# Moving the jobs that prepare sums of w2, and giving eight stores to ScalarE, in a fused attention and mixture-of-experts kernel

## The chip, the cores and the metric

One core of one Trainium2 chip. The metric is the device time of one execution in microseconds; the time of a kernel is the median over its runs. A core has five engines with a queue of instructions each: TensorE (PE; PEld is its loading of weights), VectorE (DVE), ScalarE (ACT), GpSimd (POOL) and SyncE (SP). In this kernel SP only issues DMA transfers; GpSimd issues some as well.

## The reference

Two parts, the output of the first being the input of the second. Attention goes through 32 memory slots per head (8 batches, 8 heads, 576 rows, 64 columns); then come four experts (512 → 1024 → 512), each weighted by a probability per row.

```python
a = softmax(phi, over the sequence)
k_m = einsum('bhsm,bhsd->bhmd', a, k)
v_m = einsum('bhsm,bhsd->bhmd', a, v)
attn = softmax(q @ k_m^T / sqrt(64))
x = (attn @ v_m), heads side by side        # 4608 x 512
p = domain_probs / (sum of domain_probs + 1e-9)
for e in range(4):
    h = maximum(x @ w1[e], 0)
    out += p[:, e:e+1] * (h @ w2[e])
```

## The kernel before

**Precision.** Every fp32 operand of a matmul is split into two parts: ScalarE copies (rounds) the high one, and DVE or GpSimd subtracts to get the low one. A product is then three matmuls. In the trace these splits are `L156`/`L157` (w1, w2, v), `L351`/`L352` (k and v), `L659`/`L661` (the hidden block `h`).

**Stages.** The batches are taken in four pairs. The product x·w1 is not formed from x: v_m·w1 (`vw`, L560/L562) is formed per head and expert, and the transposed attention `AT` is multiplied by it. Pairs 0 and 1 run as 256 steps, 128 to a pair (`PAIR`), 32 to an expert. A step makes one hidden block and uses another:

```python
for s in range(a, b):
    accumulate()
    run_plan(s)
    first(s + AHEAD)
    second(s)
```

`first` (L647 to L661) makes the hidden block of two steps later: matmuls, the rectified high part on ScalarE (L659), the low part on DVE (L661). `second` (L680 to L682) multiplies the step's block by a block of w2. `run_plan(s)` runs whatever was put at step s with `at(s, ...)`: the attention of later batches, the splits of the next expert's weights, loads and stores. Pairs 2 and 3 run afterwards as 64 units in another scheme with seven products in place of eight; these need sums and differences of the quadrants of w2, split in two parts.

**Order.** Steps 0 to 35 are ordered by the compiler's scheduler. From step 36 (`FREE`) on the order is that of the code: on every engine an instruction stands where `run_plan` wrote it, and an engine executes its instructions in that order.

**The jobs.** Eight jobs (one for each expert and half of its hidden width; `JOBS`, function `sums`) prepare those quadrant sums during the steps. A job at step s has SP load two blocks of w2 of 512 KB into a tile `raw` (L208), DVE form the sums from step s+3 on (L231 to L234), ScalarE copy the high parts into `sv` (L220) and GpSimd subtract the low ones (L221), four of each; and GpSimd issue four stores to memory (L226). The jobs have no tiles of their own. They borrow the attention's: `raw` lies in the tile of tag "a" and `sv` in those of "tl" and "ph", except job 5, which takes one of three "AT" tiles and one of the "kvs" tiles. A tile is handed on when its last user is done; the next job's load therefore waits for the previous job's stores.

**Keeping w2.** `keep_w2(e, j)` stores the split blocks of w2 (512 KB each) at steps 20 to 27 of every expert in the first pair (L184, issued by GpSimd); the second pair loads them back (`load_w2`, L193, issued by SP, `w<-kw` in the trace).

**Attention of batch b** (`ATT`): the first number is the step of the load of phi, the second the step in which v_m is written.

Throughout, "job n" counts from 0, "P+61" is step 61 of the second pair, and `kw` and `v` in the order are the stores' places in memory.

Of the kernel before, what the change touches and what calls it, by code (L numbers as in the profile page):

```python
# [9 lines left out]
F32 = mybir.dt.float32  # L10
# [8 lines left out]
N, DM, E, F = 4608, 512, 4, 1024  # L19
P = 128  # L20
# [8 lines left out]
PAIR = E * STEPS  # L29
# [26 lines left out]
    4: (PAIR, PAIR + 35, (PAIR + 34, PAIR + 37, PAIR + 41), (PAIR + 38, PAIR + 42, PAIR + 45)),  # L56
    5: (PAIR + 26, PAIR + 53, (PAIR + 76, PAIR + 80, PAIR + 84), (PAIR + 112, PAIR + 113, PAIR + 114)),
    6: (PAIR + 40, PAIR + 67, (2 * PAIR + 23, 2 * PAIR + 27, 2 * PAIR + 31), (2 * PAIR + 29, 2 * PAIR + 33, 2 * PAIR + 37)),
    7: (PAIR + 62, PAIR + 88, (2 * PAIR + 98, 2 * PAIR + 102, 2 * PAIR + 106), (2 * PAIR + 115, 2 * PAIR + 116, 2 * PAIR + 117)),
}  # L60

UNITS_1 = (1, 5, 5, 6, 5, 6, 8, 9, 10, 11, 11, 12, 17, 13, 13, 20)
# [7 lines left out]
UNITS = (NG - SEVEN) * E * 2 * 4  # L70
Q = 256
X_BANK, Y_BANK, AB_BANK = 4, 2, 6
JOBS = (62, 87, 99, 108, 117, PAIR + 28, PAIR + 85, PAIR + 94)
KEEP_AT, W2_AGAIN = 20, 24
FOUR_AT_7 = ((0, 4, 8, 12), (16, 20, 24, 28))
VW_LOAD_7 = ((21, 37), (26, 41))
# [4 lines left out]
def body(ctx: ExitStack, tc: tile.TileContext, qm, qt, kv, kvt, phi, prob, w1, w1d, w2, out):  # L81
    nc = tc.nc
    pool = lambda name, **k: ctx.enter_context(tc.tile_pool(name=name, bufs=1, **k))
    const, wp, work, att = pool("const"), pool("wp"), pool("work"), pool("att")
    dram = pool("dram", space=DRAM)
# [67 lines left out]
    w1t, w2t = {}, {}  # L153
# [19 lines left out]
        w2t[k, e, j] = t  # L173

    kept_for = {}
    leaving = []

    def leave(key, t):
        leaving.append((key, t))

    def leave_now():
        for key, t in leaving:
            kept_for[key] = dram.tile([P, 2, DM], F32, name="k" + "".join(map(str, key)))
            nc.gpsimd.dma_start(kept_for[key], t.bitcast(F32))  # L184
        leaving.clear()

    def keep_w2(e, j):
        leave(("w2", e, j), w2t[0, e, j])
        leave_now()

    def load_w2(k, e, j):
        t = wp.tile([P, 2, DM], F32R, name="w2", tag="w2", bufs=NJ + 1)
        nc.sync.dma_start(t.bitcast(F32), kept_for["w2", e, j])  # L193
        w2t[k, e, j] = t

    def sums(s, own, e, fh):

        kept = []
        top, low = slice(0, Q), slice(Q, DM)
        sub, v = nc.vector.tensor_sub, nc.vector  # L200

        def load():
            tag = {"tag": "a"} if own else {"tag": "AT", "bufs": 3}
            t = att.tile([P, 2, 2, DM], F32R, name="raw", **tag)
            kept.extend(t[:, i].bitcast(F32) for i in range(2))
            kept.append(t)
            for i in range(2):
                nc.sync.dma_start(kept[i], w2[e, 2 * fh + i])  # L208

        def high(i, j):  # L210
            if j == 0:
                if own and i:
                    t = att.tile([P, 2, 640], F32R, name="sv", tag="ph")
                    t = t.rearrange("p a c -> p (a c)")[:, :2 * DM].rearrange("p (a c) -> p a c", a=2)
                elif own:
                    t = att.tile([P, 2, DM], F32R, name="sv", tag="tl")
                else:
                    t = att.tile([P, 2, DM], F32R, name="sv", tag="kvs", bufs=KVS)
                kept.append(t)
            nc.scalar.copy(kept[3 + i][:, j], kept[i][:, j])  # L220
            nc.gpsimd.tensor_sub(kept[2][:, i, j], kept[i][:, j], kept[3 + i][:, j].bitcast(F32))  # L221

        def store(i):
            d = dram.tile([P, 2, 2, DM], F32, name=f"v{e}{fh}{i}")
            for r, src in enumerate((kept[3 + i], kept[2][:, i])):
                nc.gpsimd.dma_start(d[:, :, r], src.bitcast(F32))  # L226
            for j in range(2):
                kept_for["v", e, fh, 2 * i + j] = d[:, j]

        at(s, load)  # L230
        at(s + 3, lambda: v.tensor_add(kept[1][:, :, low], kept[0][:, :, low], kept[1][:, :, low]))  # L231
        at(s + 3, lambda: sub(kept[0][:, :, low], kept[0][:, :, top], kept[0][:, :, low]))
        at(s + 4, lambda: sub(kept[0][:, :, top], kept[1][:, :, low], kept[0][:, :, top]))
        at(s + 4, lambda: sub(kept[1][:, :, top], kept[1][:, :, top], kept[0][:, :, top]))  # L234
        for i in range(2):
            for j in range(2):
                at(s + 4 + 2 * i + j, lambda i=i, j=j: high(i, j))
            at(s + 6 + 2 * i, lambda i=i: store(i))

    def units_w1(e, fh, g):  # L240
        kept = []
# [468 lines left out]
    def at(s, unit):  # L710
        plan[s].append(unit if isinstance(unit, tuple) else (None, unit))
# [76 lines left out]
    for k in range(NG):  # L788
        for e in range(E):
            s = k * PAIR + e * STEPS  # L790
# [34 lines left out]
    for e in range(E):  # L825
        for j in range(NJ):
            at(e * STEPS + KEEP_AT + j, lambda a=(e, j): keep_w2(*a))
    for n, s in enumerate(JOBS):
        sums(s, s != PAIR + 28, n // 2, n % 2)
    for s in FIRST_LOADS:  # L830
        at(s, lambda: load_part(wp.tile([P, 2, DM], F32R, name="w2", tag="w2", bufs=NJ + 1)))

# [17 lines left out]
    for block in range(UNITS // 4):  # L850
        e, fh = divmod(block % (2 * E), 2)
# [428 lines left out]
```

## Time and profile before

| | us |
|---|---|
| runs | 1407.55, 1407.58, 1413.63 |
| median | 1407.58 |
| the profiled execution | 1409.54 |
| its span | 1407.4 |
| TensorE busy in it | 1366.8 |
| VectorE busy | 837.9 |
| ScalarE busy | 624.8 |
| GpSimd busy | 621.4 |
| mean granted TensorE clock | 0.994 of full speed |

The span runs from the first to the last instruction of the profiled execution; its own time is 2.1 us longer, and the median of the runs is 2.0 below that. Steps 0 to 255 end at about 800 us; the 64 units fill the rest. A row of the timeline has the start in us, the duration (of a run of alike instructions, as "x8" tells, the stretch), the engine, the line, the operation, what is written and read with shapes, and in brackets the idle time of the engine before it with what ended it. `SPq` and `POOL ... DMA` rows are the issuing of transfers, not the transfers. A row of a window has its bounds and length, the busy time of PE, PEld, DVE, ACT and POOL with counts, the granted clock, the busy share of the DMA engines and GB/s.

### The profile page before, as it was taken

The page shows a single profiled execution, that of the slowest core. Times are in us where ns is not written, and L with a number is a line of the kernel's source. Part 1 is how long each engine was busy: PE and PEld are TensorE (multiplying, and loading weights), DVE is VectorE, ACT ScalarE, POOL GpSimd, SP SyncE. Part 2 cuts the span into 40 slices and gives each one's busy share as a digit, 9 for nine tenths or more (in the row PEclk, how much of TensorE's full clock was granted, in tenths as well). Part 3 has the DMA queues.
Part 4 walks back from the last instruction along what each step waited for, and adds up shares of the span by engine and source line. Part 5 has one row for each costly group of instructions (what it writes and reads, how often), then busy time and mean ns, then how long its engine had stood idle before and what let it go on. Part 6 is the DMA issues. An engine that isn't in the chain of part 4 may idle for free.

```text
span 1407.4 us, 25235 instructions
## 1 busy us (share of the span) xinstructions
PE 1366.8 (97%) x8894; PEld 1250.2 (89%) x8894; DVE 837.9 (60%) x1894; ACT 624.8 (44%) x1536; POOL 621.4 (44%) x660
## 2 busy tenths in 40 slices
PE   7899999999999999999979999999999999999998
PEld 6688888888878888889868999899999999999998
DVE  7775545446754365354434467777667666666665
ACT  7654555433444364463225354555543333333332
POOL 4410344755552334422245276676763334333333
PEclk9999999999999999999989999999999999999999
DMA  7832327799684264444588898999985776666662
GB/s 252 272 104 84 123 85 246 228 354 318 226 313 163 90 226 145 139 140 124 188 272 292 278 311 289 314 315 331 321 306 154 223 190 179 177 180 177 178 177 80
DMA packets 102029, 301.37 MB, mean 214 GB/s; under 512 B 24976, under 2 KB 26128, under 8 KB 101904
## 3 DMA queue, kind: packets, MB, share of 16 engines
q1 hardware_dynamic: 81168, 224.26, 51.3%
q0 software_dynamic: 20736, 75.51, 13.8%
q8 instruction: 71, 1.16, 0.4%
q14 instruction: 54, 0.44, 0.1%
HBM read 213.46 MB, written 84.93 MB: 212 GB/s over the span
## 4 chain that ended last, share of the span: by engine, by line
PE 58%; DMA 1%; DVE 1%; ACT 0%; issue 0%; POOL 0%; SPq 0%; DVEq 0%; ACTq 0%
PE banks L1008 22%; PE banks L922 5%; PE banks L923 5%; PE banks L924 5%; PE banks L682 3%; PE banks L680 3%; PE banks L681 3%; PE banks L585 2%; PE banks L647 2%; PE banks L648 2%; PE banks L649 2%; PE banks L1046 1%; PE banks L1047 1%; PE banks L1048 1%; PE banks L469 1%; PE banks L363 1%
## 5 line engine op out<-in xcount | busy, mean ns | idle before, releaser
L1026 DVE SCALAR_TENSOR_TENSOR acc<-banks,pt,acc 128x256 f32<-128x256 f32 x416 | 200.0, 481 | 108.9 <-PE banks L1008 105.2
L157 POOL TENSOR_TENSOR w<-stage,w 128x512 fp32r<-128x512 f32 x134 | 176.6, 1323 | 166.0 <-ACT w L156 153.9
L682 PE MATMUL banks<-w,h 128*128 128x512 f32 x512 | 201.9, 395 | 14.3 <-DVE h L661 14.3
L661 DVE SCALAR_TENSOR_TENSOR h<-banks,h 128x256 fp32r<-128x256 f32 x256 | 107.6, 420 | 164.3 <-ACT h L659 101.6
L680 PE MATMUL banks<-w,h 128*128 128x512 f32 x512 | 202.2, 395 | 1.7 <-DVE acc L702 1.3
L681 PE MATMUL banks<-w,h 128*128 128x512 f32 x512 | 201.7, 394 | 0.0
L659 ACT ACTIVATE h<-banks 128x256 fp32r<-128x256 f32 x256 | 97.8, 384 | 193.1 <-PE banks L649 152.2
L647 PE MATMUL banks<-AT,vw 128*128 128x256 f32 (+1 forms) x512 | 157.4, 308 | 5.7 <-ACT kvs L351 2.2
L1008 PE MATMUL banks<-w,a 128*128 128x256 f32 x1080 | 154.6, 282 | 0.3 <-DVE acc L1026 0.2
L648 PE MATMUL banks<-AT,vw 128*128 128x256 f32 (+1 forms) x512 | 151.7, 297 | 0.0
L922 PE MATMUL banks<-AT,vw 128*128 128x256 f32 (+1 forms) x512 | 151.6, 296 | 0.0
L649 PE MATMUL banks<-AT,vw 128*128 128x256 f32 (+1 forms) x512 | 151.2, 296 | 0.1
L923 PE MATMUL banks<-AT,vw 128*128 128x256 f32 (+1 forms) x512 | 151.1, 295 | 0.0
L924 PE MATMUL banks<-AT,vw 128*128 128x256 f32 (+1 forms) x512 | 150.9, 295 | 0.0
L1008 PEld LDWEIGHTS banks<-w,a 128*128 128x128 f32 x1080 | 143.6, 188 | 4.9 <-issue 0.9
L989 POOL TENSOR_TENSOR vt<-ph,vt 128x512 fp32r<-128x512 f32 x64 | 84.1, 1314 | 107.3 <-ACT vt L988 78.3
L682 PEld LDWEIGHTS banks<-w,h 128*128 128x128 f32 x512 | 96.5, 189 | 37.4 <-DVE h L661 16.0
L352 POOL TENSOR_TENSOR kvs<-stage,kvs 128x512 fp32r<-128x512 f32 x58 | 75.8, 1325 | 101.4 <-ACT kvs L351 100.9
L647 PEld LDWEIGHTS banks<-AT,vw 128*128 128x128 f32 x512 | 97.1, 190 | 18.0 <-DVE vw L562 4.0
L680 PEld LDWEIGHTS banks<-w,h 128*128 128x128 f32 x512 | 96.6, 189 | 13.7 <-DVE acc L702 1.8
L681 PEld LDWEIGHTS banks<-w,h 128*128 128x128 f32 x512 | 96.6, 189 | 11.0
L156 ACT CAST w<-stage 128x512 fp32r<-128x512 f32 x168 | 102.7, 619 | 6.3 <-DMA stage<-in_w 4.1
(149 smaller groups left out, 2985.6 us busy)
## 6 DMA issues: line engine op xcount, KB each, us to landing
w<-kw SPq DMA_DIRECT2D x93, 512.0 KB, 5.3
vwd<-vst POOLq DMA_DIRECT2D x80, 512.0 KB, 6.2
vw<-vwd SPq DMA_DIRECT2D x320, 128.0 KB, 5.7
w<-v SPq DMA_DIRECT2D x55, 512.0 KB, 5.5
stage<-in_w SPq DMA_DIRECT2D x44, 512.0 KB, 4.3
stage<-in_w1d SPq DMA_DIRECT2D x40, 512.0 KB, 4.7
stage<-in_kv SPq DMA_DIRECT2D x32, 512.0 KB, 3.9
kw<-w POOLq DMA_DIRECT2D x32, 512.0 KB, 6.7
```

The lines of the kernel that those rows point to most:

```text
L157: eng.tensor_sub(dst[:, 1, :], raw, dst[:, 0, :].bitcast(F32))
L647: nc.tensor.matmul(ps, w[:, 0, f], at_t[:, g, 0, c], start=g == 0, stop=False)
L648: nc.tensor.matmul(ps, w[:, 0, f], at_t[:, g, 1, c], start=False, stop=False)
L649: nc.tensor.matmul(ps, w[:, 1, f], at_t[:, g, 0, c], start=False, stop=g == 1)
L680: nc.tensor.matmul(po[t], x[:, 0, :], w[:, 0, :], start=j == 0, stop=False)
L681: nc.tensor.matmul(po[t], x[:, 0, :], w[:, 1, :], start=False, stop=False)
L682: nc.tensor.matmul(po[t], x[:, 1, :], w[:, 0, :], start=False, stop=j == NJ - 1)
L922: nc.tensor.matmul(ps, w[:, 0, f], at_t[:, g, 0, c], start=g == 0, stop=False)
L923: nc.tensor.matmul(ps, w[:, 0, f], at_t[:, g, 1, c], start=False, stop=False)
L924: nc.tensor.matmul(ps, w[:, 1, f], at_t[:, g, 0, c], start=False, stop=g == 1)
L1008: nc.tensor.matmul(ps, a[:, l, jj], w[:, r, c], start=start and jj + i == 0, stop=jj == 1 and i == 2, skip_group_check=True,)
L1026: VE.scalar_tensor_tensor(a, src, p, a, ALU.mult, ALU.add)
```

## The change

Every job gets three numbers: its step, the home of its `raw` tile, and the distance from the load to the first sum (3 before, now 4 for all but one).

| job | load before | sums from | load now | sums from |
|---|---|---|---|---|
| 0 | 62 | 65 | 62 | 66 |
| 1 | 87 | 90 | 86 | 90 |
| 2 | 99 | 102 | 97 | 101 |
| 3 | 108 | 111 | 108 | 112 |
| 4 | 117 | 120 | 118 | 122 |
| 5 | P+28 | P+31 | P+26 | P+30 |
| 6 | P+85 | P+88 | P+61 | P+64 |
| 7 | P+94 | P+97 | P+87 | P+91 |

Job 6 takes "a" for `raw` and a "kvs" tile for `sv`. The attention of batch 7 starts two steps later. The stores of expert 0's w2 blocks are issued by ScalarE, those of the other experts by GpSimd as before.

```diff
-    7: (PAIR + 62, PAIR + 88, (2 * PAIR + 98, 2 * PAIR + 102, 2 * PAIR + 106), (2 * PAIR + 115, 2 * PAIR + 116, 2 * PAIR + 117)),
+    7: (PAIR + 64, PAIR + 90, (2 * PAIR + 98, 2 * PAIR + 102, 2 * PAIR + 106), (2 * PAIR + 115, 2 * PAIR + 116, 2 * PAIR + 117)),
...
-JOBS = (62, 87, 99, 108, 117, PAIR + 28, PAIR + 85, PAIR + 94)
+JOBS = (
+    (62, "", 4), (86, "", 4), (97, "", 4), (108, "", 4), (118, "", 4),
+    (PAIR + 26, "AT", 4), (PAIR + 61, "a", 3), (PAIR + 87, "", 4),
+)
...
     def keep_w2(e, j):
-        leave(("w2", e, j), w2t[0, e, j])
-        leave_now()
+        d = kept_for["w2", e, j] = dram.tile([P, 2, DM], F32, name=f"kw{e}{j}")
+        (nc.gpsimd if e else nc.scalar).dma_start(d, w2t[0, e, j].bitcast(F32))
...
-    def sums(s, own, e, fh):
+    def sums(s, home, lag, e, fh):
...
         at(s, load)
-        at(s + 3, lambda: v.tensor_add(kept[1][:, :, low], kept[0][:, :, low], kept[1][:, :, low]))
-        at(s + 3, lambda: sub(kept[0][:, :, low], kept[0][:, :, top], kept[0][:, :, low]))
...
+        s += lag
+        at(s, lambda: v.tensor_add(kept[1][:, :, low], kept[0][:, :, low], kept[1][:, :, low]))
+        at(s, lambda: sub(kept[0][:, :, low], kept[0][:, :, top], kept[0][:, :, low]))
...
         for i in range(2):
             for j in range(2):
-                at(s + 4 + 2 * i + j, lambda i=i, j=j: high(i, j))
-            at(s + 6 + 2 * i, lambda i=i: store(i))
+                at(s + 1 + 2 * i + j, lambda i=i, j=j: high(i, j))
+            at(s + 3 + 2 * i, lambda i=i: store(i))
```

After line 80 or so the new file is six or seven lines shorter, so a statement of the old L208 is L201 in the new order, L193 is L186, L184 is L182, L226 is L219, L221 is L214, L624 is L618, L157 is L160.

**SP, the last expert of the second pair (about P+93 to P+104).** `w<-kw` are the loads of w2's kept blocks, `vw<-vwd` loads of v_m·w1, `raw<-in_w` the job's load. Before:

```order
L624 DMA vw<-vwd_2889 32x1024
L624 DMA vw<-vwd_2918 32x1024
L193 DMA w_6947<-kw_4088 128x1024
L193 DMA w_6967<-kw_4115 128x1024
L208 DMA raw<-in_w 128x1024 x2
L193 DMA w_6987<-kw_4150 128x1024
L624 DMA vw<-vwd_2950 32x1024
```

Now:

```order
L618 DMA vw<-vwd_2889 32x1024
L618 DMA vw<-vwd_2918 32x1024
L448 DMA vs<-vh 64x2x32 x8
L186 DMA w_6960<-kw_4086 128x1024
L186 DMA w_6979<-kw_4108 128x1024
L186 DMA w_7002<-kw_4143 128x1024
L618 DMA vw<-vwd_2950 32x1024
```

and some twenty rows further up, where job 6's load stood before:

```order
L618 DMA vw<-vwd_2918 32x1024
L145 DMA stage<-in_w1d 128x1024
L201 DMA raw<-in_w 128x1024 x2
L186 DMA w_6825<-kw_3964 128x1024
L186 DMA w_6846<-kw_3991 128x1024
```

Job 7's load left the place between the last blocks of w2 and stands ahead of the first of them; the reading of batch 7's v_m (`vs<-vh`) came in two steps later.

**GpSimd, steps 112 to 120 (jobs 3 and 4).** `L157`/`L160` is the split of a block of w2, `L221`/`L214` a job's subtraction, the `v_` rows a job's stores. Before:

```order
L221 TENSOR_TENSOR raw<-raw,sv 128x512
L226 DMA v_3898<-sv 256x1x512
L226 DMA v_3898<-raw 256x1x512
L221 TENSOR_TENSOR raw<-raw,sv 128x512 x2
L157 TENSOR_TENSOR w_3963<-stage,w_3963 128x512
L184 DMA kw_3966<-w_3304 128x1024
L226 DMA v_3968<-sv 256x1x512
L226 DMA v_3968<-raw 256x1x512
L157 TENSOR_TENSOR w_3991<-stage,w_3991 128x512
L184 DMA kw_3994<-w_3332 128x1024
```

Now:

```order
L214 TENSOR_TENSOR raw<-raw,sv 128x512 x2
L219 DMA v_3929<-sv 256x1x512
L219 DMA v_3929<-raw 256x1x512
L214 TENSOR_TENSOR raw<-raw,sv 128x512
L160 TENSOR_TENSOR w_3961<-stage,w_3961 128x512
L182 DMA kw_3964<-w_3304 128x1024
L214 TENSOR_TENSOR raw<-raw,sv 128x512
L160 TENSOR_TENSOR w_3988<-stage,w_3988 128x512
L182 DMA kw_3991<-w_3332 128x1024
L219 DMA v_3993<-sv 256x1x512
L219 DMA v_3993<-raw 256x1x512
```

Job 3's second pair of stores stands behind one more split and one more store of a kept block.

**ScalarE, about steps 20 to 24 of the scheduled part.** `kw_` rows are the stores of expert 0's blocks, which stood in GpSimd's queue. Now:

```order
L182 DMA kw_1187<-w_363 128x1024
L274 ACTIVATE ph,zs<-ph,nm 128x576
L554 CAST vw<-banks 64x512 x2
L483 ACTIVATE at<-at 128x512
L285 ACTIVATE ph<-ph,zs 128x576
L345 CAST kvs<-stage 128x512
L286 COPY ph<-ph 128x64
```

Before, the same stretch has no DMA:

```order
L280 ACTIVATE ph,zs<-ph,nm 128x576
L560 CAST vw<-banks 64x512
L351 CAST kvs<-stage 128x512 x2
L291 ACTIVATE ph<-ph,zs 128x576
L351 CAST kvs<-stage 128x512
L292 COPY ph<-ph 128x64
```

The store stands ahead of the exponential of phi, and the scheduler's order of the casts around it is another.

More of the change, by code (lines that the diff above doesn't have):

```diff
@@ L175, in body @@
     kept_for = {}
[L176 to L185, printed above, removed]
     def keep_w2(e, j):
-        leave(("w2", e, j), w2t[0, e, j])
-        leave_now()
+        d = kept_for["w2", e, j] = dram.tile([P, 2, DM], F32, name=f"kw{e}{j}")
+        (nc.gpsimd if e else nc.scalar).dma_start(d, w2t[0, e, j].bitcast(F32))
     def load_w2(k, e, j):
@@ L202, in load @@
         def load():
-            tag = {"tag": "a"} if own else {"tag": "AT", "bufs": 3}
+            tag = {"tag": "AT", "bufs": 3} if home == "AT" else {"tag": "a"}
             t = att.tile([P, 2, 2, DM], F32R, name="raw", **tag)
@@ L211, in high @@
             if j == 0:
-                if own and i:
+                if not home and i:
                     t = att.tile([P, 2, 640], F32R, name="sv", tag="ph")
                     t = t.rearrange("p a c -> p (a c)")[:, :2 * DM].rearrange("p (a c) -> p a c", a=2)
-                elif own:
+                elif not home:
                     t = att.tile([P, 2, DM], F32R, name="sv", tag="tl")
@@ L230, in sums @@
         at(s, load)
-        at(s + 3, lambda: v.tensor_add(kept[1][:, :, low], kept[0][:, :, low], kept[1][:, :, low]))
-        at(s + 3, lambda: sub(kept[0][:, :, low], kept[0][:, :, top], kept[0][:, :, low]))
-        at(s + 4, lambda: sub(kept[0][:, :, top], kept[1][:, :, low], kept[0][:, :, top]))
-        at(s + 4, lambda: sub(kept[1][:, :, top], kept[1][:, :, top], kept[0][:, :, top]))
+        s += lag
+        at(s, lambda: v.tensor_add(kept[1][:, :, low], kept[0][:, :, low], kept[1][:, :, low]))
+        at(s, lambda: sub(kept[0][:, :, low], kept[0][:, :, top], kept[0][:, :, low]))
+        at(s + 1, lambda: sub(kept[0][:, :, top], kept[1][:, :, low], kept[0][:, :, top]))
+        at(s + 1, lambda: sub(kept[1][:, :, top], kept[1][:, :, top], kept[0][:, :, top]))
         for i in range(2):
             for j in range(2):
-                at(s + 4 + 2 * i + j, lambda i=i, j=j: high(i, j))
-            at(s + 6 + 2 * i, lambda i=i: store(i))
+                at(s + 1 + 2 * i + j, lambda i=i, j=j: high(i, j))
+            at(s + 3 + 2 * i, lambda i=i: store(i))
     def units_w1(e, fh, g):
@@ L827, in body @@
             at(e * STEPS + KEEP_AT + j, lambda a=(e, j): keep_w2(*a))
-    for n, s in enumerate(JOBS):
-        sums(s, s != PAIR + 28, n // 2, n % 2)
+    for n, job in enumerate(JOBS):
+        sums(*job, n // 2, n % 2)
     for s in FIRST_LOADS:
```

## The prediction

> **What bounds the kernel now.** I read the page's totals first, then the list of what PE (TensorE) waited for, then windows by stage.
>
> ```profile
> span 1407.4 us, 25235 instructions
> PE 1366.8 (97%) x8894; PEld 1250.2 (89%) x8894; DVE 837.9 (60%) x1894; ACT 624.8 (44%) x1536; POOL 621.4 (44%) x660
> ```
> ```profile
> PE banks L682 <- DVE h L661: 14.3, 4, 9.9
> ...
> PE banks L647 <- ACT kvs L351: 2.2, 1, 2.2
> ...
> PE banks L585 <- POOL w L157: 0.9, 1, 0.9
> ```
> ```profile
> 0.00:75.00 75.00, 60.63 (x356) 52.11 (x357) 57.17 (x125) 50.62 (x119) 35.85 (x41) 0.95 0.75 259
> ...
> 300.00:426.00 126.00, 120.56 (x685) 103.61 (x684) 74.45 (x149) 50.74 (x124) 63.05 (x68) 1.00 0.84 306
> 426.00:700.00 274.00, 271.49 (x1570) 238.53 (x1569) 131.84 (x326) 125.95 (x344) 89.54 (x77) 1.00 0.44 146
> 700.00:730.00 30.00, 20.10 (x101) 17.18 (x100) 7.43 (x15) 6.48 (x17) 9.72 (x10) 0.83 0.90 273
> ```
>
> TensorE is busy 97% of the span; 1407.4 − 1366.8 = 40.6 us is all the idle time there is, and its work is the same before and after. So the change can only be worth a part of that idle, plus slow clock behind it. The waits are written as total, times, longest: the largest single one is 9.9 us, on the second half of a split hidden block (`h`, DVE, L661). The windows (length, then busy time of PE, PEld, DVE, ACT, POOL, granted clock, DMA share, GB/s) place it: 700–730 has 9.9 us of idle and a mean clock of 0.83, while 426–700 loses only 2.5 us in 274. The start (0–75) loses 14.4 us, most of it before the kernel can begin.
>
> **The stall at 709–719: job 7.** The timeline there:
>
> ```profile
> 698.12 0.69 POOL L226 DMA_DIRECT2D v<-raw  x1 [2.29 <-issue]
> ...
> 702.28 0.38 ACT L659 ACTIVATE h<-banks 128x256 fp32r<-128x256 f32 x1 [1.70 <-PE banks L649]
> ...
> 704.37 0.38 ACT L659 ACTIVATE h<-banks 128x256 fp32r<-128x256 f32 x1 [1.70 <-PE banks L649]
> ...
> 707.12 0.89 SPq L193 DMA_DIRECT2D w<-kw  x2
> ...
> 708.24 1.82 SPq L208 DMA_DIRECT2D raw<-in_w  x2
> ...
> 710.16 0.38 SPq L193 DMA_DIRECT2D w<-kw  x1
> ...
> 717.07 0.69 DVE L231 TENSOR_TENSOR raw<-raw 128x512 f32<-128x512 f32 x1 [13.94 <-DMA raw<-in_w]
> ...
> 718.87 0.79 PE L682 MATMUL banks<-w,h 128*128 128x512 f32 x1 [9.90 <-DVE h L661]
> ```
> ```profile
> 713.50:718.90 5.40, 0.03 (x1) 0.03 (x1) 1.80 (x4) 0.00 (x0) 0.00 (x0) 0.50 1.05 329
> 718.90:723.70 4.80, 4.80 (x14) 4.06 (x15) 2.48 (x5) 3.09 (x7) 3.42 (x4) 0.50 0.77 217
> 723.70:728.00 4.30, 4.30 (x25) 3.79 (x24) 0.50 (x2) 1.50 (x5) 4.30 (x5) 0.99 0.65 244
> ```
>
> Job 7's two blocks of w2 are issued by SP at 708.24 and DVE gets them only at 717.07. DVE runs in the written order, so it stood 13.94 us in front of the first sum, with the next step's L661 behind it; PE stood 9.90 us. The difference, 13.94 − 9.90 = 4.0 us, is how much of a DVE wait these steps hide. The load came late because its tile is job 6's `raw`, whose last store was issued at 698.12, and because it stood behind other loads in SP's queue. When PE resumed, the clock read 0.50 for another 4.8 us: half of that, 2.4 us, was lost. Price of the stall: 9.9 + 2.4 = **12.3 us**.
>
> After, job 7's load is issued seven steps earlier, in the place in SP's queue that job 6's load has now (the order above shows it behind the same w1d load), and job 6 itself goes away to P+61. The steps are 704.37 − 702.28 = 2.09 us long, and the sums stand at P+91 instead of P+97, so load and sums have 4 steps = 8.4 us between them. Job 7's own load took from 708.24 to 717.07, 8.8 us, under a DMA share of 1.05; with the 4.0 us hidden there is room for 12.4 us. I take the stall as gone: **−12.3**.
>
> **What is late next there.** The loads of expert 3's second matrix (`w<-kw`, blocks 5, 6 and 7) are issued at 707.12 and 710.16. Their times to landing, and below them that of job 6's last store:
>
> ```profile
> DMA to landing us min/median/max: 5.9/6.6/9.6
> ```
> ```profile
> DMA to landing us min/median/max: 4.6/4.6/4.6
> ```
>
> Without the stall the steps that use them would begin at 712.7, 714.8 and 716.9 (702.28 plus 5, 6, 7 steps of 2.09). They land 5.9 to 9.6 us after issue: 713.0, about 714, and 719.8 for the last, which stood behind the 1.82 us of job 7's load and shared the engines with its megabyte. Without job 7's load in front it would be issued by 708.4 and be there by 715. So block 5 is 0.3 us late if nothing else changes; the ends are 0 and 3 (all three keep their times, 719.8 − 716.9). Beside them job 7's load of 1 MB goes away, and its stores of 2 MB come before them: the written steps are P+94 and P+96, some 699 to 704, and job 6's last one took 4.6 us to land, so they are out of the way by about 708. I take **+0.4**, near the lower end.
>
> **Jobs 3 and 4, and the load of phi behind them.**
>
> ```profile
> 393.00 0.85 POOL L226 DMA_DIRECT2D v<-raw  x1
> ...
> 393.60 1.57 POOL L157 TENSOR_TENSOR w<-stage,w 128x512 fp32r<-128x512 f32 x1
> ...
> 398.00 1.69 SPq L208 DMA_DIRECT2D raw<-in_w  x2
> 399.83 0.38 ACT L659 ACTIVATE h<-banks 128x256 fp32r<-128x256 f32 x1 [2.40 <-PE banks L649]
> ...
> 402.62 0.38 ACT L659 ACTIVATE h<-banks 128x256 fp32r<-128x256 f32 x1 [2.40 <-PE banks L649]
> ...
> 408.20 0.69 DVE L231 TENSOR_TENSOR raw<-raw 128x512 f32<-128x512 f32 x1 [5.55 <-DMA raw<-in_w]
> ...
> 410.01 0.50 PE L682 MATMUL banks<-w,h 128*128 128x512 f32 x1 [2.11 <-DVE h L661]
> ```
>
> The same chain, smaller: job 3's last store (393.00) lands, job 4's load goes at 398.00, 5.0 us after that issue; DVE has it at 408.20, 10.2 us later; DVE waits 5.55, PE 2.11, so 3.44 is hidden. After, DVE comes to job 4 two steps later, 4.2 to 5.6 us by the two cadences shown (2.09 and 402.62 − 399.83 = 2.79): 402.65 + 4.9 = 407.5, and PE stalls only if the load lands after about 411. But GpSimd's order puts one more split (1.57) and one more store's issue (0.6) ahead of job 3's stores, and the step itself is later: the load is issued 2 to 3 us later, at about 400.5, and lands at 409 to 411. I take a rest of 0.5 (ends 0 and 2.1): −2.1 + 0.5 = **−1.6**.
>
> Job 4's own last stores also go later, and phi of batch 4 loads into one of the tiles that they empty:
>
> ```profile
> 430.61 0.82 SPq L266 DMA_DIRECT2D ph<-in_phi  x2
> ...
> 433.59 0.75 DVE L271 TENSOR_REDUCE nm<-ph 128x1 f32<-128x576 f32 x1 [2.19 <-DMA ph<-in_phi]
> ```
>
> Its first reader already waits 2.19 on DVE with no stall of PE. The stores move by one step against PE (up to 2.8 us), so the wait becomes 2.2 to 5.0; against 3.4 to 4.0 hidden, PE stalls 0 to 1.6. I take **+0.7**.
>
> **Jobs 5 and 6, jobs 0 to 2.**
>
> ```profile
> 537.51 0.59 ACT L531 CAST AT<-banks 128x512 fp32r<-128x512 f32 x1 [3.00 <-DMA v<-raw]
> ...
> 541.55 0.62 PE L363 MATMUL banks<-kvs,a 128*128 128x256 f32 x3 [0.50 <-POOL kvs L352]
> ...
> 621.91 0.46 POOL L157 TENSOR_TENSOR vh<-v,vh 128x128 fp32r<-128x128 f32 x1 [16.43 <-ACT vh L156]
> ```
>
> Job 5 stands two steps earlier but with one more step for its load: its stores land earlier, and ScalarE's 3.00 us wait for its `AT` tile with the 0.50 us on PE behind it should go: **−0.5**. Job 6 falls into the 16.43 us in which GpSimd does nothing before 621.91, and its tile `a` is not wanted for nine steps after: **0**. If that cover were gone (its load late), PE would lose what exceeds 4.0 of DVE's wait; a load of 8.8 us in 3 steps of 2.09 would make DVE wait 2.5, which is hidden. Jobs 0 to 2 move by one or two steps; the only stall near them is the 0.9 on a split of w1 by GpSimd (L585), which stands behind job 0's two subtractions and stores: between −0.9 and +1.3 (one more subtraction ahead of it), I take **−0.3**.
>
> **Stores of the first expert by ScalarE.** Eight stores leave GpSimd's queue and enter ScalarE's, in steps whose order the scheduler chooses. The median of a store's time to landing, and the rows:
>
> ```profile
> kw<-w POOLq DMA_DIRECT2D x32, 512.0 KB, 6.7
> ```
> ```profile
> 34.38 0.33 SPq L142 DMA_DIRECT2D stage<-in_w  x1
> ...
> 35.44 1.75 POOL L184 DMA_DIRECT2D kw<-w  x3
> ...
> 45.09 1.14 ACT L337 CAST tl<-stage 128x512 fp32r<-128x512 f32 x2 [3.10 <-DMA stage<-in_kvt]
> ...
> 46.88 0.39 PE L647 MATMUL banks<-AT,vw 128*128 128x256 f32 x1 [1.21 <-ACT vw L560]
> ```
>
> GpSimd gives 8 × 0.58 = 4.7 us for their issue; SP, the nearest row to a ScalarE issue, takes 0.33, so ScalarE gives 8 × 0.33 = 2.6. PE's stalls in these steps on ScalarE are 1.21 (46.88) and 2.2 (L351): at best they go (−3.4), at worst all issue time comes onto the path (+2.6). Each store must also wait until both parts of its block are written, and the scheduler put them behind other ScalarE work. I take the middle, **−0.5**, for a term that I cannot place. A DMA row here is at 0.75 of the engines on average. The Trainium skill ("DMA: Bandwidth & Descriptors", "Issuing engines are not separate DMA queues") says that transfers started by any engine share the same 16 DMA engines and that issuing from several engines saves only issue time. By it this part gives no bandwidth: the term would be 0 to +2.6 and the sum 0.5 to 3.1 us higher. The trace of before has no store by ScalarE to weigh it with.
>
> **Sum.** −12.3 + 0.4 − 1.6 + 0.7 − 0.5 + 0 − 0.3 − 0.5 = −14.1 us. The profiled execution took 1409.5, so 1395.4 there. The median of the runs, 1407.6, lies 2.0 below it: **1393.5**.
>
> The clock is in this sum only behind the long stall. The Trainium skill ("TensorE: Matmul & The Clock Gate", "What's actually happening") has the array's clock halve after an idle window of about 3.4 us and recover after as much busy time; the trace agrees in kind (0.50 within the 9.9 us stall, for 4.8 us after it). By it a remaining stall of over 3.4 us would cost about 2 us on top; none of the terms is that long.
>
> **Rivals.**
> - *New waits in the place of the old* (1397 to 1403). The last loads of expert 3 stay late by 3, phi's wait costs 1.6, job 4 keeps 2.1, and one of the shifted jobs makes a stall of 3 with its slow clock of 2. For it: DMA share is 0.84 and 0.90 in the two stretches, and all landings there are 6 to 10 us. Against it: 1 MB of load leaves the stretch in which they are slow, and the cover is 3.4 to 4.0 each time. +4 to +9 on the forecast.
> - *The early steps lose* (1396 to 1402). ScalarE in its order carries 2.6 us more, the scheduler deals steps 3 to 35 anew, and all of 0–75 loses 14.4 us already. +3 to +8. Against it: GpSimd has 4.7 us less.
> - *Slower than before* (1410 and up). A store at the head of ScalarE's queue waits for its block, or for its turn, and everything behind it stops. By the 45.09 and 46.88 rows a ScalarE wait of 3.10 cost PE 1.21, so 1.9 is hidden; eight such waits of 6.7 (a store's time to landing) would cost 8 × 4.8 = 38. It decides from a mean wait of 1.9 + 14.1 / 8 = 3.7 us each. Against it: the scheduler places them after the splits that they need.
> - *Job 7 stays late* (about 1405): the load, though earlier, waits again for the tile, so that the gain is only 2. Against it: the tile's former owner is now 26 steps away.
>
> **Chances.** Forecast 0.62 (1389.5 to 1397), new waits 0.17, early loss 0.10, slower 0.04, job 7 still late 0.03, more gain (the ScalarE waits in the first 75 us go too) 0.04. A measurement here can tell 0.5% from no change, 7 us: faster means under 1400.5. About 0.7 of the second and third cases lie there: 0.62 + 0.04 + 0.7 × 0.27 = 0.85, a little less for sizes I may have missed, 0.84; same 0.12, slower 0.04. The range 1389 to 1403 takes in the best ends of all terms and both middle rivals.
>
> **What would show it.** The group "PE on DVE h L661" falls from 14.3 to under 2; the clock in 700–730 is 1.00 and PE is busy for nearly all of it; job 7's first sum on DVE shows a wait under 4. At 400–412 PE idles under 1 us. The ScalarE wait for `v<-raw` is gone. In 0–75 PE's busy time is 59 to 63. Wrong would be: a wait of PE on `w<-kw` over 3 us near the start of expert 3, a new DVE wait on `raw` over 4 anywhere, or ScalarE rows with several microseconds of idle ahead of its stores.

## The result and the profile after

The changed kernel takes 1398.52 us in the median of 6 runs (1395.84 to 1399.56), the one before 1409.97 in 6 runs beside them. The ratio is 0.9915, 95% interval 0.9898 to 0.9933: 12 us faster (9 to 14). The profiled execution took 1398.29 us, against 1409.54 before: 11.2 us less. Of all executions below one, of e1_jobs, took 2687.89 us, nearly twice the others of its kernel, and is in no ratio.

The totals of the profile after, and the head of the list of what TensorE waited for (total, times, longest). Line numbers are now those of the new file, most of them six lower:

```profile
span 1396.2 us, 25220 instructions
...
PE 1365.6 (98%) x8894; PEld 1250.9 (90%) x8894; DVE 838.1 (60%) x1894; ACT 625.5 (45%) x1536; POOL 617.2 (44%) x652
```
```profile
PE banks L514 <- DVE at L493: 4.8, 2, 2.8
...
PE banks L676 <- DVE h L655: 1.9, 1, 1.9
PE banks L641 <- DVE h L655: 1.8, 1, 1.8
PE banks L535 <- DVE h L655: 1.5, 1, 1.5
```

The 14.3 us on `h` have become 5.2 in three waits, and a new one stands at the head: 4.8 on the softmax `at`, 2.1 of it new. The windows by stage:

```profile
0.00:75.00 75.00, 61.62 (x382) 53.66 (x382) 58.28 (x129) 52.24 (x127) 31.46 (x33) 0.98 0.74 258
...
300.00:426.00 126.00, 119.40 (x652) 102.53 (x651) 71.54 (x144) 47.76 (x118) 59.14 (x63) 0.96 0.79 286
426.00:700.00 274.00, 270.62 (x1567) 238.22 (x1566) 135.63 (x332) 128.78 (x350) 93.68 (x82) 1.00 0.47 157
700.00:730.00 30.00, 30.00 (x166) 26.36 (x165) 11.45 (x26) 10.96 (x30) 11.49 (x13) 1.00 0.97 291
```

700–730 is full, at clock 1.00 (20.1 busy at 0.83 before). 300–426 is worse than before: 119.4 busy where it was 120.6, and a clock of 0.96 that was 1.00. To place the time exactly, I took the start of each step's first matmul with `h` (L680 before, L674 after) in both traces:

| stretch | before | after | change |
|---|---|---|---|
| before step 0 | 35.0 | 34.8 | −0.2 |
| steps 0 to 35 | 125.9 | 121.1 | −4.8 |
| steps 36 to 127 | 265.3 | 271.2 | +5.9 |
| second pair, to its last step | 371.7 | 359.6 | −12.1 |
| the rest, to the end of the span | 609.6 | 609.5 | −0.1 |

So the gain at job 7 is there, the start brought nearly 5 us more, and steps 36 to 127 took them away again.

**The place of the old stall.** Timeline of job 7 after, and then the times to landing of the last three loads of w2:

```profile
677.09 0.83 SPq L201 DMA_DIRECT2D raw<-in_w  x2
```
```profile
691.44 0.42 DVE L655 SCALAR_TENSOR_TENSOR h<-banks,h 128x256 fp32r<-128x256 f32 x1 [1.68 <-ACT h L653]
691.78 0.68 DVE L225 TENSOR_TENSOR raw<-raw 128x512 f32<-128x512 f32 x1
```
```profile
DMA to landing us min/median/max: 4.8/5.3/7.5
```

The load is issued 14.7 us before its first sum, which starts without a wait. The loads of w2 land in 4.8 to 7.5 us (5.9 to 9.6 before), and TensorE has no wait in 700–730.

**The new loss at step 103.** Timeline of the whole change:

```profile
336.94 0.80 SPq L201 DMA_DIRECT2D raw<-in_w  x2
...
342.82 0.69 DVE L225 TENSOR_TENSOR raw<-raw 128x512 f32<-128x512 f32 x1 [2.23 <-DMA raw<-in_w]
...
348.23 1.19 DVE L493 TENSOR_TENSOR at<-at,z 64x256 f32<-64x256 f32 x1
...
349.48 0.33 PE L514 MATMUL banks<-ident,at 64*128 64x64 f32 x2 [2.08 <-DVE at L493]
...
349.74 3.37 PE L463 MATMUL banks<-kT,stage 128*128 128x64 f32 x16
```
```profile
350.00:356.50 6.50, 6.50 (x27) 6.11 (x27) 2.27 (x6) 1.17 (x4) 2.13 (x3) 0.51 0.94 321
```

DVE waits 2.23 us for job 2's load, its sums follow, the softmax behind them (L493) is late, TensorE stops for 2.08 us, and then the clock reads 0.51 for 6.5 us. By the starts of steps 103 and 105, together 5.3 us. The load had been written two steps earlier, but it was not issued earlier against the steps. Before, it stood here:

```profile
342.08 0.80 SPq L208 DMA_DIRECT2D raw<-in_w  x2
```

That is 5.1 us later than now, and steps 97 to 103 began 5.2 to 5.5 us later as well. In both kernels SP waited for job 1's last store from the tile, 3.0 us before and 3.9 now; job 1's sums stand at step 90 in both. So only job 2's sums came forward, by one step, and the load did not.

**Job 4.** It was to lose its stall; it has one of 1.45 and 0.34, and slow clock behind it:

```profile
400.90 1.72 SPq L201 DMA_DIRECT2D raw<-in_w  x2
...
404.97 0.42 DVE L655 SCALAR_TENSOR_TENSOR h<-banks,h 128x256 fp32r<-128x256 f32 x1 [1.68 <-ACT h L653]
...
411.08 0.69 DVE L225 TENSOR_TENSOR raw<-raw 128x512 f32<-128x512 f32 x1 [5.69 <-DMA raw<-in_w]
...
412.89 0.50 PE L535 MATMUL banks<-w,vt 128*128 128x512 f32 x1 [1.45 <-DVE h L655]
...
414.20 0.39 PE L641 MATMUL banks<-AT,vw 128*128 128x256 f32 x1 [0.34 <-DVE vw L556]
```
```profile
415.00:418.50 3.50, 3.50 (x11) 2.73 (x9) 2.29 (x4) 3.43 (x8) 1.98 (x2) 0.52 1.01 397
```

At P+33 a wait of 1.82 us on `h` has come, where before there were 0.44 there and 0.50 at P+40; the load of phi makes VectorE wait 1.75 us (2.19 before) and TensorE not at all.

### The profile page after: what moved, and what is told of

Read it like the earlier page. It is cut to its first block, busy times and chain, and to the rows that moved or that the text cites. A ratio compares the mean times of both kernels' runs of the same rounds, so it can differ in the third digit from the quotient of the medians.

```text
span 1396.2 us, 25220 instructions
## 1 busy us (share of the span) xinstructions
PE 1365.6 (98%) x8894; PEld 1250.9 (90%) x8894; DVE 838.1 (60%) x1894; ACT 625.5 (45%) x1536; POOL 617.2 (44%) x652
## 4 chain that ended last, share of the span: by engine, by line
PE 73%; DVE 3%; DMA 3%; POOL 2%; issue 1%; ACT 1%; SPq 0%; DVEq 0%; POOLq 0%; ACTq 0%
PE banks L1002 22%; PE banks L674 6%; PE banks L675 6%; PE banks L676 6%; PE banks L916 5%; PE banks L917 5%; PE banks L918 5%; PE banks L641 3%; PE banks L642 3%; PE banks L643 3%; PE banks L579 2%; PE banks L463 2%; PE banks L357 1%; PE banks L1040 1%; PE banks L1041 1%
## 5 line engine op out<-in xcount | busy, mean ns | idle before, releaser
L160 POOL TENSOR_TENSOR w<-stage,w 128x512 fp32r<-128x512 f32 x134 | 176.6, 1319 | 191.2 <-ACT w L159 180.9
L674 PE MATMUL banks<-w,h 128*128 128x512 f32 x512 | 203.0, 396 | 1.4 <-DVE acc L696 1.3
L674 PEld LDWEIGHTS banks<-w,h 128*128 128x128 f32 x512 | 96.8, 189 | 13.7 <-DVE acc L696 1.7
```

The lines of the kernel that those rows point to most:

```text
L160: eng.tensor_sub(dst[:, 1, :], raw, dst[:, 0, :].bitcast(F32))
L674: nc.tensor.matmul(po[t], x[:, 0, :], w[:, 0, :], start=j == 0, stop=False)
```

## The experiments

All times in one table; each ratio is to the runs of the kernel before on the same chip. The last column is (1 − ratio) × 1411.

| run | median us | ratio, interval | us under before |
|---|---|---|---|
| the whole change | 1398.5 | 0.9915 (0.9898 to 0.9933) | 12.0 |
| e1_jobs | 1404.5 | 0.9949 (0.9935 to 0.9963) | 7.2 |
| e2_stores | 1405.2 | 0.9966 (0.9952 to 0.9980) | 4.8 |
| e3_jobs67 | 1399.0 | 0.9911 (0.9882 to 0.9940) | 12.6 |
| e4_job2 | 1394.4 | 0.9887 (0.9867 to 0.9908) | 15.9 |
| e5_retimed | 1392.0 | 0.9865 (0.9847 to 0.9884) | 19.0 |
| e6_sp | 1399.1 | 0.9916 (0.9898 to 0.9934) | 11.9 |
| e7_act18 | 1397.8 | 0.9902 (0.9886 to 0.9919) | 13.8 |
| e8_phi | 1388.1 | 0.9847 (0.9824 to 0.9869) | 21.6 |
| e9_early2 | 1401.9 | 0.9942 (0.9922 to 0.9961) | 8.2 |
| e10_pool | 1396.2 | 0.9893 (0.9878 to 0.9907) | 15.1 |
| e11_nostore | 1390.8 | 0.9852 (0.9835 to 0.9868) | 20.9 |

### The moved jobs alone, and the stores alone

```diff
# e1_jobs, against the changed kernel
-        (nc.gpsimd if e else nc.scalar).dma_start(d, w2t[0, e, j].bitcast(F32))
+        nc.gpsimd.dma_start(d, w2t[0, e, j].bitcast(F32))
# e2_stores, against the changed kernel: the old steps and distances, and ATT[7] as before
+JOBS = ((62, "", 3), (87, "", 3), (99, "", 3), (108, "", 3), (117, "", 3),
+        (PAIR + 28, "AT", 3), (PAIR + 85, "", 3), (PAIR + 94, "", 3))
```

> The moved jobs alone; expert 0's stores stay with GpSimd. In the two traces the change gained 4.9 us in steps 0 to 9, lost 5.9 us from step 96 to the end of the first pair, and gained 12.4 us at P+99. Theory A (the early gain is the ScalarE stores): this run keeps the start of before, PE busy about 60.6 in 0-75, and is 6 to 7 us faster than before (1403 to 1404). Rival B (the early difference is only a start that varies from run to run): as fast as the whole change, 11 to 12 us under before.

> The ScalarE stores alone, all jobs as before. Theory A: 4 to 6 us faster than before, all of it within the first 75 us, the stall of 9.9 at 709 still there. Rival B: no difference from before (under 2 us).

7.2 us and 4.8 us: they add up to the 12.0 of the whole change, and theory A holds for both. In the profile of the stores alone the old stall is still there:

```profile
PE banks L676 <- DVE h L655: 15.6, 3, 11.6
```

What the start does is read from one window, 35 to 155 us (busy PE of 120 us). Before, the whole change, the moved jobs alone, the stores alone:

```profile
35.00:155.00 120.00, 112.93 (x636) 94.90 (x635) 86.67 (x190) 70.91 (x171) 26.03 (x25) 1.00 0.47 157
```
```profile
35.00:155.00 120.00, 116.45 (x663) 99.17 (x663) 88.95 (x195) 73.38 (x176) 23.41 (x18) 1.00 0.49 160
```
```profile
35.00:155.00 120.00, 112.34 (x626) 94.44 (x625) 86.47 (x188) 70.82 (x171) 27.57 (x26) 0.99 0.47 155
```
```profile
35.00:155.00 120.00, 116.05 (x664) 98.97 (x663) 89.41 (x194) 73.55 (x176) 24.09 (x19) 1.00 0.47 158
```

112.3 to 112.9 with the stores on GpSimd, 116.1 to 116.5 with them on ScalarE. These are two executions of each; another with the stores on GpSimd has 115.85 (e10_pool below). The lists of TensorE's waits tell which stops went: with the stores on GpSimd it waits in steps 2 to 6 for what ScalarE makes, 1.21 us on `vw` and 2.17 on `kvs` before, 1.03 and 1.96 in e1_jobs. With the stores on ScalarE no wait on ScalarE is left in these steps, and 0.81 and 0.43 at step 3, on DVE's `vw`, have come (the whole change).

### Jobs 6 and 7 alone

```diff
# e3_jobs67, against e2_stores; the stores on GpSimd
-        (PAIR + 28, "AT", 3), (PAIR + 85, "", 3), (PAIR + 94, "", 3))
+        (PAIR + 28, "AT", 3), (PAIR + 61, "a", 3), (PAIR + 87, "", 4))
-    7: (PAIR + 62, PAIR + 88,
+    7: (PAIR + 64, PAIR + 90,
```

> Only jobs 6 and 7 (and batch 7's attention with them) moved; jobs 0 to 5 and all stores as before. Theory A (job 7's stall is worth its 9.9 us and 2.4 us of slow clock): 12 to 13 us faster than before, PE without a wait over 1 us in 600-730. Rival (the loads of w2 behind it take its place): 8 to 10 faster, with PE waiting for w<-kw.

12.6 us (interval 8.5 to 16.6), as much as the whole change brings. The window 700–730 of this run:

```profile
700.00:730.00 30.00, 30.00 (x166) 26.35 (x165) 10.96 (x26) 10.81 (x29) 12.02 (x13) 1.00 0.98 290
```

So moving jobs 0 to 5 costs what the stores gain: 12.6 for jobs 6 and 7 alone, 7.2 for all the jobs.

### Where jobs 0 to 5 lose: job 2 one step later

```diff
# e4_job2, against the changed kernel
-    (62, "", 4), (86, "", 4), (97, "", 4), (108, "", 4), (118, "", 4),
+    (62, "", 4), (86, "", 4), (98, "", 4), (108, "", 4), (118, "", 4),
```

> The whole change, with job 2 one step later (98, so that its sums stand at step 102 as before). Theory C (the loss of 5.3 us at steps 103 and 104 is one stall of 2.1 us, caused by job 2's sums standing in front of the softmax of step 103, and the half clock after it): the stall and the slow clock go, 4 to 5.5 us faster than the whole change (about 1393 to 1394). Rival D (job 2's late load, or the crowding of that place, makes the stall wherever it stands): within 2 us of the whole change.

15.9 against 12.0 us under before: about 4 of the 5 us come back, as theory C had it, though the intervals of the two ratios still overlap. In its timeline the two matmuls of the late softmax have no wait in front of them, and the scores that follow run in 2.00 us instead of 3.37:

```profile
349.19 0.33 PE L514 MATMUL banks<-ident,at 64*128 64x64 f32 x2
349.46 2.00 PE L463 MATMUL banks<-kT,stage 128*128 128x64 f32 x16
```

The same trace shows the next stall, at step 76, and the clock behind it:

```profile
270.00 0.47 PE L579 MATMUL banks<-w,vs 128*128 128x512 f32 x1 [1.49 <-ACT h L653]
```
```profile
271.00:275.00 4.00, 3.95 (x13) 3.49 (x14) 2.04 (x6) 2.04 (x7) 3.96 (x5) 0.57 0.70 174
```

### The late load or the sums themselves: job 2's load early, its sums in place

```diff
# e9_early2, against the changed kernel
-    (62, "", 4), (86, "", 4), (97, "", 4), (108, "", 4), (118, "", 4),
+    (62, "", 4), (83, "", 5), (95, "", 6), (108, "", 4), (118, "", 4),
```

> The whole change, with job 2's load early and its sums where they are (load at step 95, distance 6, sums at 101); for that job 1 is three steps earlier (83, distance 5, sums at 88). It parts the two readings of the stall at step 103. C1 (DVE came late to the softmax because it stood 2.2 us in front of job 2's load): with the load early DVE does not wait, the stall of 2.1 and the slow clock go, 4 to 5 us faster than the whole change (about 1394). C2 (the four sums, 2.8 us of DVE, are themselves too much in front of that softmax): the stall at step 103 stays at 1 to 2 us.

As to step 103 it was C1. Job 2's load now lands 8 us before its sums; the first sum starts at 345.42 without a wait, and TensorE's stop in front of the softmax falls from 2.08 to 0.42:

```profile
352.69 0.34 PE L514 MATMUL banks<-ident,at 64*128 64x64 f32 x2 [0.42 <-DVE at L493]
```

But the run is slower than the whole change, not faster (8.2 against 12.0 under before), so the number expected for it failed. Another wait takes the place at step 95, for the load of q, and 4 us of clock at 0.6 follow it:

```profile
328.32 2.24 PE L463 MATMUL banks<-kT,stage 128*128 128x64 f32 x16 [3.34 <-DMA stage<-in_qm]
```

That load stands on the edge in several of these kernels: TensorE waited for it 3.0 us in e7_act18 and 2.4 in e10_pool, and not in the whole change. From issue to landing it took 6.5 us here, 7.9 and 7.1 in those two, and 4.8 to 5.6 in the other ten traces; here it was also issued 2.0 us later against the steps than in the whole change. No run tells whether job 1's earlier stores did that.

### Three more places retimed

```diff
# e5_retimed, against e4_job2
-    (62, "", 4), (86, "", 4), (98, "", 4), (108, "", 4), (118, "", 4),
-    (PAIR + 26, "AT", 4), (PAIR + 61, "a", 3), (PAIR + 87, "", 4),
+    (62, "", 3), (86, "", 4), (98, "", 4), (108, "", 4), (118, "", 5),
+    (PAIR + 26, "AT", 5), (PAIR + 61, "a", 3), (PAIR + 87, "", 4),
# e8_phi, besides
-    4: (PAIR, PAIR + 35,
+    4: (PAIR + 1, PAIR + 35,
```

> The run with job 2 at 98, and three more places: job 0 with distance 3 again (its stores one step earlier), job 4 with distance 5 (sums at 123), job 5 with distance 5 (sums at P+31, as before, with the earlier load). Theory: each stall is DVE or a store coming at the wrong step. Job 0's late stores hold up the store of vst behind them (1.5 us at step 76 in two traces); job 4's sums stand 5.7 us in front of a load that lands at 411 (1.8 us of PE and 1.7 of slow clock); job 5's sums at P+30 cost 1.8 at P+33. All three gone: 3 to 6 us under the run with job 2 at 98, 1388 to 1391. Rival: job 4's stores, a step later, hold up the load of phi for batch 4, and its first reader stops PE at P+3 by 1 to 3 us: 1390 to 1394, with a DVE wait for ph of over 4 us.

19.0 under before, 3 more than with job 2 alone: the low end of the theory, and by its time in the rival's range, since the rival is true as well. The stalls at steps 76 and 123 and most of that at P+33 are gone from the trace (a new one at step 125 is 0.77), but job 4's stores now go one step later, and the load of phi behind them stops TensorE:

```profile
429.14 0.75 DVE L265 TENSOR_REDUCE nm<-ph 128x1 f32<-128x576 f32 x1 [4.73 <-DMA ph<-in_phi]
```
```profile
431.60 0.50 PE L676 MATMUL banks<-w,h 128*128 128x512 f32 x1 [1.40 <-DVE h L655]
```

4.73 of wait, 1.40 of stall: 3.3 hidden, which fits the 3.4 and 4.0 of before.

> The retimed run (jobs 0, 2, 4 and 5), with the attention of batch 4 begun one step later (P+1). Theory: the stall of 1.4 us that the late load of phi now makes at P+5 goes, since its first reader on VectorE comes 2.1 us later and the stores before it do not move: DVE's wait for ph falls from 4.7 to under 3, 1 to 2 us faster than the retimed run (about 1390). Rival: the load itself is written a step later in SyncE's queue and lands later by as much; the wait stays at 4 to 5 and the time within 1 us.

1388.1 us, 21.6 under before and 2.6 under e5_retimed, somewhat more than the 1 to 2 expected; this is the fastest of the kernels that do all the work. DVE's wait for phi is 2.60 and nothing of TensorE waits for it:

```profile
427.91 0.75 DVE L265 TENSOR_REDUCE nm<-ph 128x1 f32<-128x576 f32 x1 [2.60 <-DMA ph<-in_phi]
```

### Why the stores on ScalarE help

```diff
# e6_sp, against e4_job2
-        (nc.gpsimd if e else nc.scalar).dma_start(...)
+        (nc.gpsimd if e else nc.sync).dma_start(...)
# e7_act18, against e4_job2: for expert 0 at steps 18 to 25
-            at(e * STEPS + KEEP_AT + j, lambda a=(e, j): keep_w2(*a))
+            at(e * STEPS + KEEP_AT + j + (0 if e else -2), lambda a=(e, j): keep_w2(*a))
# e10_pool, against e8_phi: nc.gpsimd for all experts
# e11_nostore, against e10_pool
+        if e == 0 and j:
+            kept_for["w2", e, j] = kept_for["w2", 0, 0]
+            return
```

> The run with job 2 at 98, with expert 0's eight stores issued by SyncE in place of ScalarE. GpSimd's order is then that of the whole change, but TensorE's order in steps 3 to 35 is that of before save one place. Theory E (the early gain comes from GpSimd being free of the stores): the start is as fast as with ScalarE, PE busy about 61.6 in 0-75, total within 1.5 us of the run with job 2 at 98. Rival F (the gain comes from the other order that the scheduler gives TensorE, VectorE and ScalarE when the stores are ScalarE's): the start is that of before, with PE waits on kvs (about 2), vw (about 1) and h, 4 to 6 us slower than the run with job 2 at 98. Rival G: SyncE waits at the stores and its loads come later still: over 6 us slower.

> The run with job 2 at 98, with expert 0's stores written two steps earlier (18 to 25), still issued by ScalarE; the scheduler gives TensorE a slightly different order (14 rows). Theory E and the plain form of F (any order with the stores on ScalarE): the early gain stays, within 1.5 us of the run with job 2 at 98. Rival: the gain hangs on one particular order, and 2 to 5 us are lost in steps 0 to 9.

> The best run so far (jobs 0, 2, 4, 5 and batch 4's phi retimed) with expert 0's stores back on GpSimd; TensorE's order in steps 3 to 35 is then that of before. E and F both say that the early gain is lost: 4 to 6 us slower than the best run, about 1393. Rival: without the later stalls the early one shrinks too, under 2 us.

> The run with the stores on GpSimd, but seven of the eight stores of expert 0 left out (the second pair loads the one block eight times, so its result differs); TensorE's order stays that of before. E (the gain is GpSimd and the DMA engines being free of the stores): as fast at the start as with ScalarE's stores, PE's loss in steps 0 to 35 about 7, some 4 to 6 us under the run with all stores on GpSimd. F (the gain is the other order that the scheduler makes): within 1.5 us of the run with all stores on GpSimd, PE's loss there 10 to 13.

By the times: SyncE 4 us slower than e4_job2 (11.9 against 15.9), as rival F had it; ScalarE two steps earlier 2.1 us slower than e4_job2 (13.8), more than the 1.5 expected though the intervals overlap, its start unchanged and its loss in the wait for q at step 95; GpSimd in the best kernel 6.5 us slower (15.1 against 21.6), somewhat more than expected; with seven of the eight stores left out 5.8 us faster than that, which looks like E. But the times mix in other places. In the window of the start, SyncE, then GpSimd in the best kernel, then without seven stores:

```profile
35.00:155.00 120.00, 114.68 (x649) 96.55 (x648) 89.25 (x193) 72.40 (x174) 23.64 (x18) 1.00 0.49 157
```
```profile
35.00:155.00 120.00, 115.85 (x656) 97.34 (x655) 88.72 (x193) 72.92 (x175) 28.56 (x27) 1.00 0.47 157
```
```profile
35.00:155.00 120.00, 115.88 (x657) 98.23 (x658) 89.21 (x193) 72.24 (x174) 23.85 (x19) 1.00 0.39 128
```

The kernel before, e1_jobs, e3_jobs67 and e10_pool have the same instructions in the same order on every engine up to step 36, and lost 7.1, 7.7, 7.5 and 4.2 of these 120 us. With the stores on ScalarE, in the orders that the scheduler makes for them (one in six kernels, another in e7_act18), the loss was 3.0 to 4.0 in seven executions. Between 115.85 with the stores on GpSimd and 115.88 without seven of them there is nothing; so E is not shown. What e11_nostore gained on e10_pool lay elsewhere, 1.9 us ahead of step 0 and about 5 at step 95, where it has no wait for q. In the best kernel more than half of GpSimd's loss lay there too: of 8.9 us between the profiles of e8_phi and e10_pool 3.4 stand at step 36 (1.6 of them ahead of step 0), and 4.7 come with the wait for q and the clock behind it:

```profile
331.30 3.17 PE L463 MATMUL banks<-kT,stage 128*128 128x64 f32 x16 [2.45 <-DMA stage<-in_qm]
```

What can be said: with ScalarE's stores comes an order of the first 36 steps that loses little, each time; the order of before loses about as much (4.2) or up to 4 us more, from one execution to the next. How much of that is the order and how much the transfers beside it stays open. No run had ScalarE's order with GpSimd's stores.

## Why the prediction was right, and where its steps were off

The time came out in the range (1389 to 1403), and on the side that was forecast, but not where the sum had it: 1398.5 against 1393.5, outside the 1389.5 to 1397 to which the forecast gave 0.62. Of the 5.0 us some 2.4 are the base, a median before of 1407.58 in the three runs known then and of 1409.97 in six; some 2.6 are the sum. That the sum is so near is luck in good part: the two terms that were off most, jobs 0 to 2 by +5.0 and the stores by −4.3, nearly cancel, and without the stores the same moves take 1404.5 (e1_jobs), outside the range. Term by term, by the starts of the steps in the two profiles:

| term | forecast | profiles |
|---|---|---|
| job 7's stall | −12.3 | −12.4 |
| loads of w2 behind it | +0.4 | 0 |
| job 6 in its new place | 0 | 0 |
| job 5 | −0.5 | +0.3 |
| jobs 3 and 4 | −1.6 | +1.2 |
| phi of batch 4 | +0.7 | 0 |
| jobs 0 to 2 | −0.3 | +4.7 |
| stores on ScalarE | −0.5 | −4.8 |
| sum | −14.1 | −11.0 |

- **Job 7: right**, step and size; the run with jobs 6 and 7 alone shows it by itself (12.6 us). The price had to hold the slow clock as well as the 9.9 us of stall.
- **Job 4: wrong sign.** The step that failed is "DVE comes to job 4 two steps later, 4.2 to 5.6 us". DVE came 2.7 later (405.4 instead of 402.65), because it does not keep TensorE's steps: before, it was held up at step 120 by the sums into `acc` and `accm` until 402.6 (last row of them below), after, at 122, it came straight from the step's `h`. The load landed at the late end of what was forecast, 411.0, DVE waited 5.7, and 3.9 were hidden. To that came 1.7 of slow clock after a stall shorter than the 2.11 of before, which had cost none.

```profile
401.90 0.74 DVE L702 SCALAR_TENSOR_TENSOR accm<-banks,pt,accm 128x512 f32<-128x512 f32 x1
```

- **Jobs 0 to 2: the term that was mis-sized most.** They were priced by the one stall that already stood near them, 0.9. What stands on DVE behind the moved sums (the softmax of step 103) had no term, and neither had what holds the load back (job 1's last store). One step for job 2's sums turned a load that came in time into one that DVE waited 2.23 us for; the run with the load early and the sums in place took most of that stall away (0.42 of 2.08 stayed).
- **Job 5:** the two waits that were to go went, ScalarE's 3.00 and TensorE's 0.50 behind it; what was put at nothing is that its sums, one step earlier, would make TensorE wait 1.82 at P+33 where it had waited 0.44 (0.45 with the sums back at P+31, in e5_retimed).
- **ScalarE's stores:** −0.5 was called the middle of −3.4 and +2.6 (which is −0.4) for a term that could not be placed; the two runs of one part alone give 4.8. The best end was the nearest: the two waits on ScalarE that make up the 3.4 are gone. The Trainium skill ("DMA: Bandwidth & Descriptors", "Issuing engines are not separate DMA queues") spoke for no gain in bandwidth. The DMA share in 35–155 agrees with that, 0.47 to 0.49 whichever engine issued; but the order that the scheduler made changed with the issuer, which neither that rule nor a count of issue times could show.
- **The rivals.** New waits came, as the first rival said, and its time (1397 to 1403) is the one that was measured: not late loads of w2 or phi, but "one of the shifted jobs makes a stall of 3 with its slow clock of 2" (job 2: 2.08 and 3.4) and "job 4 keeps 2.1" (1.8, with slow clock of 1.7). What had been given 0.04, that the ScalarE waits in the first 75 us go too, came as well, with jobs 0 to 2 taking as much away. The early loss and the slower rival did not come: no wait of TensorE in the whole change is on ScalarE.

## What to carry to other kernels

Where an engine runs in a written order, a job that is moved has to be checked against what stands behind its first wait in the new place, not only against the stall that it leaves: one step decided 4 us here. A load that is written earlier is not issued earlier while its tile is still being emptied. Estimate from the trace when each engine gets to a place, since engines run ahead of or behind the steps by different amounts. A change to what an automatic scheduler orders is a new order of the whole part: measure it alone, and look at its window in several executions before giving it a cause.

## What the runs showed of the hardware that was not expected

Short stalls can cost slow clock, and need not. A stop of 1.45 and one of 0.34 us at 413 to 414 were followed by a clock of 0.52 for 3.5 us, one of 2.08 by 0.51 for 6.5 us, one of 1.49 (with 0.58 after it) by 0.57 for 4 us; in other executions 2.11 at 410 (before) and 1.40 at 431.6 (e5_retimed) had no slow clock behind them. A half clock of 3.4 us costs 1.7 us, as much as such a stall itself. It can make up most of the difference between executions of one kernel: of the 23 runs of the kernel before beside e1_jobs the slowest (1416.2) had a mean clock of 0.987 and the fastest (1406.6) of 0.993, and 0.006 of 1411 us is 8.5 of the 9.6 us, an estimate. In the six runs of e7_act18 time and clock do not go together.

The traces tell the two kinds of stop apart. In all thirteen the granted clock changes only on a grid of 3.41 us, which lies differently in each execution, and every slow stretch up to the last matmuls is one to four such windows long. Four windows of that grid from the whole change, and two from e5_retimed:

```profile
346.69:350.10 3.41, 1.33 (x9) 0.80 (x8) 3.10 (x9) 1.59 (x6) 3.41 (x4) 1.00 0.01 2
350.10:353.52 3.42, 3.42 (x17) 3.42 (x17) 1.10 (x2) 0.00 (x0) 1.68 (x2) 0.50 0.91 340
...
411.54:414.96 3.42, 1.73 (x9) 1.25 (x10) 3.29 (x7) 0.01 (x1) 0.00 (x0) 1.00 1.04 384
414.96:418.37 3.41, 3.41 (x11) 2.73 (x10) 2.19 (x4) 3.34 (x7) 1.85 (x2) 0.50 1.01 396
```
```profile
427.67:431.08 3.41, 2.52 (x14) 1.83 (x12) 1.69 (x4) 0.87 (x2) 0.00 (x0) 1.00 0.88 307
431.08:434.49 3.41, 2.90 (x15) 2.54 (x16) 1.11 (x5) 2.41 (x6) 0.00 (x0) 1.00 0.02 7
```

In the first two pairs TensorE was busy for 1.33 and 1.73 us of a window at full clock, and half clock came in the next; the stop of e5_retimed is split between two windows that stay 2.52 and 2.90 busy. Counted over all thirteen traces from 20 to 1380 us, half clock followed 19 of the 20 windows at full clock that were busy for less than 0.45, 9 of the 21 between 0.45 and 0.53 (the 2.11 of before left 0.46), and 1 of some 5100 above; that one was busy for 0.75, most of it with the narrow 128x64 products (e1_jobs, 358.27 to 361.69). This is read from the windows; no run was made to try it.

The Trainium skill ("TensorE: Matmul & The Clock Gate", "What's actually happening") gives about 3.4 us of idle for the clock to halve. By that rule, as the prediction used it, stalls of 1.4 to 2.1 us should have cost only themselves. These runs disagree on the idle time that it takes, and agree on the length of the slow stretch, 3.4 us or a whole multiple of it.
